# Consecutive tokens in a group of 128, v in four loads, and the gate's loads on ScalarE's queue

## The chip, the cores and the metric

The kernel runs on one core of a Trainium2 chip. The time is device microseconds of one execution, the median of several runs. A profile comes from a further, profiled execution, which has its own time. Engines are called as in the profile: PE (TensorE; PEld its weight loads), DVE (VectorE), ACT (ScalarE), POOL (GpSimd), SP (SyncE). A "q" behind an engine's name (SPq, ACTq) means the queue in which that engine issues DMAs.

## The reference

Linear attention over 8 batches, 8 heads, 576 tokens and 64 columns a head, followed by a mixture of experts over the 4608 tokens of 512 columns. Cut to what matters:

```python
def phi(x):                                    # q, k: (8, 8, 576, 64); w_phi: (64, 128)
    proj = np.einsum('bhsd,df->bhsf', x, w_phi)
    proj = proj - np.max(np.abs(proj), axis=-1, keepdims=True)
    return np.concatenate([np.exp(proj), np.exp(-proj)], axis=-1)
kv  = np.einsum('bhsf,bhsd->bhfd', phi(k), v)
z   = np.sum(phi(k), axis=2)
num = np.einsum('bhsf,bhfd->bhsd', phi(q), kv)
den = np.einsum('bhsf,bhf->bhs', phi(q), z)[..., None] + 1e-06
x   = (num / den).transpose(0, 2, 1, 3).reshape(4608, 512)

do_compute = x @ w_skip > 0                    # the other tokens are copied to the output
logits = x[do_compute] @ w_gate                # 8 experts, the best one is taken
e, g   = argmax(logits), softmax(logits)[argmax(logits)]
out[do_compute] = x + g * (relu(x @ w1[e]) @ w2[e])      # w1: (8, 512, 1024), w2: (8, 1024, 512)
```

All of it is in fp32; the expert products are made of a high and a low part of each operand.

## The kernel before

The attention part comes first, up to about 385 us of the profiled execution, and the expert part after it.

**Units and steps.** A unit is four heads of one batch, of k or of q: 16 units of k and 16 of q. A unit has five items: item 0 is the tail (64 tokens a head, 512 to 575), items 1 to 4 cover the 512 others, 1 and 2 for one half of the heads, 3 and 4 for the other. The main loop walks over steps; at each step the stages of several items run, some steps apart: load, transposing (`st_t`), projection with w_phi on PE (`st_proj`, L318), subtraction of the largest value on VectorE (L325, L328), the exponentials on ScalarE (L343, L344 for k; L370, L371 for q), products (L386 and L393 for k with v, L484 for q), and the division (`norm`, L435 to L448). The stream of q runs six steps behind that of k.

**Loads of q and k.** `st_load` (L265) issues four DMAs of 144 KB for a unit, all on SyncE's queue, in pieces of 32 columns (128 bytes) a token, so that 32 tokens lie on 32 partitions. There are four buffers for these tiles ("raw"); a load waits until the buffer's former unit has been transposed.

**Transposes.** VectorE transposes blocks of 32x32. Item 0 is one operation of 128x128 (L293); items 1 and 3 are one operation of 128x512 each (L295), which serve two items. 512 tokens are cut into four groups of 128. In the kernel before, group g holds the tokens 4p + g, p from 0 to 127. Therefore the 32 tokens of a block go to four groups, eight to each: neighbouring tokens are written 128 elements (512 bytes) apart. PE reads a group as 64 + 64 consecutive columns (L320).

**Where the group's order is seen elsewhere.** v must have the same tokens on the same partitions: `st_loadv` (L272) loads the four heads of a unit in one DMA, 256 consecutive elements (four tokens) for each partition and head; two buffers. The attention's result `xm` has token 4p + g in [p, g]; it is stored to the scratch rows (`rowm`, L502, L563) and, as the output of tokens that no expert computes, to the output (`rest`, L634). The table `kt_i` (L154 to L161) says which scratch row (first half) and which output row (second half) each [p, group] is.

**The gate.** `wgs` holds w_gate and w_skip in the layout of the products; GpSimd copies it into `aug` (L138), which is first used at step 10 (`st_aug`, L417). Its eight loads (L130, L131; 4.0 and 0.5 KB) are issued on SyncE's queue by `setup_aug` at step 6.

**Order.** The instructions of an engine run in the order of its queue. For the attention part, a planner of the language orders each engine's queue by times that it works out itself from the kernel; only PE's order is written out by hand from step 8 to 79 (CFG "man"). Changing instructions can thus reorder others. The expert part's order is written out by hand.

**The expert part.** Rows are gathered from the scratch rows by GpSimd (L214), multiplied with the weights of their expert (L887 to L919), and scattered to the output (L847). Which rows stand together in a slot follows from their rank within an expert, counted group by group and, in a group, partition by partition.

Of the kernel before, what the change touches and what calls it, by code (L numbers as in the profile page):

```python
# [18 lines left out]
P = 128  # L19
# [5 lines left out]
def kernel(  # L25
# [12 lines left out]
    nc = tc.nc  # L38
    B, H, S, D = q.shape
    NF = w_phi.shape[1]  # L40
    E = w_gate.shape[1]
    DM = H * D
    SQ = S
# [54 lines left out]
    wgs = ac.tile([P, NP2, E + 1], F32, name="wgs")  # L98
# [22 lines left out]

    ft = const.tile([P, NSL, 4], I32, name="ft")

    def setup_aug():
        for hd in range(2):
            r = slice(hd * 64, hd * 64 + 64)
            for hq in range(NQ):
                w = slice((hq * 4 + 2 * hd) * D, (hq * 4 + 2 * hd + 2) * D)
                g2 = slice(2 * hq, 2 * hq + 2)
                nc.sync.dma_start(out=wgs[r, g2, 0:E], in_=w_gate[w].rearrange("(g p) e -> p g e", p=D))  # L130
                nc.sync.dma_start(out=wgs[r, g2, E:E + 1], in_=w_skip[w].rearrange("(g p o) -> p g o", p=D, o=1))  # L131
        nc.gpsimd.memset(aug, 0.0)
        for hd in range(2):
            r = slice(hd * D, (hd + 1) * D)
            c = hd * NA1
            for g in range(NP2):
                nc.gpsimd.tensor_copy(out=aug[r, g, c:c + D], in_=ident[r, hd * D:(hd + 1) * D])
            nc.gpsimd.tensor_copy(out=aug[r, :, c + D:c + NA1], in_=wgs[r])  # L138

    def setup():  # L140
        nc.gpsimd.memset(ones_b, 1.0)
        nc.gpsimd.memset(ones_f, 1.0)
        nc.gpsimd.memset(Stot, 0.0)
        nc.gpsimd.affine_select(
            out=tri, in_=ones_b, pattern=[[1, P]], base=-1, channel_multiplier=-1,
            compare_op=ALU.is_ge, fill=0.0,
        )
        nc.gpsimd.iota(iota_p, pattern=[[1, P]], base=0, channel_multiplier=0, allow_small_or_imprecise_dtypes=True)
        nc.gpsimd.iota(desc, pattern=[[-1, E]], base=E, channel_multiplier=0, allow_small_or_imprecise_dtypes=True)
        nc.gpsimd.memset(ones_b, 1.0)  # L150
        NB2 = B // 2
        kt_i = const.tile([P, 2, NT], I32, name="kt_i")
        kv_ = kt_i.rearrange("p c (b t) -> p c b t", t=9)
        nc.gpsimd.iota(kv_[:, 0, :, 0:8], pattern=[[2 * S, NB2], [512, 2], [1, 4]], base=0, channel_multiplier=4)  # L154
        nc.gpsimd.iota(kv_[:, 0, :, 8:9], pattern=[[2 * S, NB2], [1, 1]], base=1024, channel_multiplier=1)
        nc.gpsimd.iota(
            kv_[:, 1, :, 0:8], pattern=[[2 * S, NB2], [S, 2], [1, 4]], base=0, channel_multiplier=4)
        for par in range(2):
            r = slice(par * 64, par * 64 + 64)
            nc.gpsimd.iota(  # L160
                kv_[r, 1, :, 8:9], pattern=[[2 * S, NB2], [1, 1]], base=par * S + 512, channel_multiplier=1)  # L161
        h_i = const.tile([P, 2, NT], I32, name="h_i")
        nc.vector.tensor_scalar(out=h_i[:, 1], in0=kt_i[:, 0], scalar1=127, scalar2=None, op0=ALU.bitwise_and)
        nc.vector.tensor_tensor(out=h_i[:, 0], in0=kt_i[:, 0], in1=h_i[:, 1], op=ALU.subtract)
        nc.vector.tensor_scalar(out=h_i[:, 1], in0=h_i[:, 1], scalar1=1.0, scalar2=None, op0=ALU.add)
        nc.vector.tensor_copy(out=sid, in_=kt_i[:, 1])
        nc.gpsimd.memset(ft[:, NS2:NSL, 1:2], 0)
        nc.gpsimd.memset(ft[:, NS2:NSL, 3:4], int(BIG))
        nc.vector.tensor_copy(out=ids.rearrange("p t c -> p c t"), in_=h_i)
# [58 lines left out]
    with actx:  # L228
# [7 lines left out]
        vu = v.rearrange("b h s d -> (b h) s d").rearrange("(u h) s d -> u s h d", h=4)  # L236
# [9 lines left out]
        for b in range(B):  # L246
            for kind in ("k", "q"):
                for hq in range(NQ):
                    u = Unit()
# [9 lines left out]
        def st_load(u):  # L259
            src = kv_in[u.kind]  # L260
            u.raw = ld.tile([P, 2, 18, 32], F32, tag="raw", name="raw", bufs=4)
            for hd in range(2):
                for dh in range(2):
                    r = hd * 64 + dh * 32
                    nc.sync.dma_start(  # L265
                        out=u.raw[r:r + 32].rearrange("p r t c -> p (r t) c"),
                        in_=src[u.g, hd][:, :, dh * 32:dh * 32 + 32])

        def st_loadv(u):
            u.v = ld.tile([P, 4, 4 * D], F32, tag="v", name="v")  # L270
            u.vt = vts[u.g % 2]
            nc.sync.dma_start(  # L272
                out=u.v.rearrange("p h (g c) -> p h g c", c=D).rearrange("p h g c -> p h (g c)"),
                in_=vu[u.g, 0:4 * P].rearrange("(p g) h c -> p h g c", g=4).rearrange("p h g c -> p h (g c)"))

        def st_loadvt(u):
            for pr in range(2):
# [4 lines left out]
        def st_t(u, i):  # L282
            if i == 0:
                n, sfx = P, "t"
                src = u.raw[:, :, 16:18, :].rearrange("p r t c -> p r (t c)")
            elif i in (1, 3):
                n, sfx = 4 * P, ""
                src = u.raw[:, i // 2, 0:16, :].rearrange("p t (q g) -> p t q g", g=4)
            else:
                return  # L290
            xT = hl.tile([P, n], F32, tag="xT" + sfx, name="xT" + sfx)
            if i == 0:
                nc.vector.transpose(out=xT.rearrange("p (r c) -> p r c", r=2), in_=src)  # L293
            else:
                nc.vector.transpose(out=xT.rearrange("p (g t q) -> p t q g", g=4, q=8), in_=src)  # L295
            u.hlp[(i + 1) // 2] = xT

        def st_proj():
# [213 lines left out]
        def post(b):  # L512
            last = b == B - 1
            xm, lgm = xm_of[b]
# [21 lines left out]
            for xx, lg, o, n in reversed(parts):  # L536
                nc.vector.tensor_reduce(
                    out=L[:, o:o + n, :], in_=lg.rearrange("p t h e -> p t e h"), axis=AX.X, op=ALU.add,
# [5 lines left out]
                out=key[:, 0:nt], in0=d[:, 0:nt], scalar=0.0,  # L544
# [6 lines left out]
                out=OH[:, T, :], in0=L[:, 0:nt, E:E + 1].broadcast_to([P, nt, E]), scalar=0.0, in1=oh[:, 0:nt],  # L551
# [5 lines left out]
            for xx, lg, o, n in parts:  # L557
                nc.scalar.activation(
                    out=xx[:, :, DM + 1:XW], in_=sid[:, t0 + o:t0 + o + n].rearrange("p (t o) -> p t o", o=1), func=AF.Copy)
# [11 lines left out]
            S = 4  # L571
# [60 lines left out]

            def rest():
                nc.sync.dma_start(  # L634
                    out=out[b * SQ:b * SQ + 4 * P].rearrange("(p g) m -> p g m", g=4), in_=xm[:, :, 0:DM])
                if b % 2 == 1:
                    for par in range(2):
                        o = (b - 1 + par) * SQ + 4 * P
                        nc.sync.dma_start(out=out[o:o + 64], in_=xt[par * 64:par * 64 + 64, 0, 0:DM])

            if last:
                rests.extend((rank, rest))
            else:
                for d, f in zip(CFG["post"], (rank, index, rest)):
                    later.append((now[0] + d, f))
                if b == EB:
                    for j in range(2):
                        later.append((now[0] + CFG["post"][2] + 1 + 2 * j, lambda j=j: pick(j)))
# [49 lines left out]
        for dh in range(2):  # L698
            nc.scalar.dma_start(
                out=wsrc[dh * 64:dh * 64 + 64],  # L700
                in_=w_phi)
        st_load(streams[0][1][0])

        def run_stage(lag, f):
            for items, us, off in streams:
                s = now[0] - off - lag
                if 0 <= s < n:
                    f(*items[s])
# [7 lines left out]
        def f_t():  # L716
            for items, us, off in streams:
                s = now[0] - off
                if s == CFG["ql"]:
                    st_load(us[0])  # L720
                if 0 <= s < n:
                    u, i = items[s]
                    st_t(u, i)
                    if i == 0 and s // 5 + 1 < len(us):
                        st_load(us[s // 5 + 1])
# [360 lines left out]
    def weight_regs(e):  # L1086
        r = nc.sync.value_load(e, min_val=0, max_val=E - 1)
        return bass.ds(r, 1)
# [5 lines left out]
    for grp in CFG["seq"]:  # L1094
# [7 lines left out]
        for which, w, n in how:  # L1102
            for _ in range(n):
                x = slots[which]
                c = done.get((x, w), 0)
# [42 lines left out]
    def step_at(t):  # L1148
        return sum(1 for v in T if v < t)
# [29 lines left out]
    for xs_, back in ((two, 2), (one, 1)):  # L1179
        for n, x in enumerate(xs_):  # L1180
            if x not in order[0:2]:
                free = end[xs_[n - back]] + LATE + 1 if n >= back else 0
                g = free if x[0] == "E" else max(free, made)
                at(g, lambda x=x: gather(x))
                r = max(step_at(T[g] + 8.0), step_at(T[begin[x]] - CFG["rows"]), one_done[order[order.index(x) - 2]] + 1)
                at(min(r, begin[x] - 1), lambda x=x: rows(x))
    loose[0] = True
    with tc.manual_schedule():
# [4 lines left out]
        for k, (w, x, c) in enumerate(steps):  # L1193
            kind, i = x
# [53 lines left out]
    with tc.For_i(0, nx, 1) as it:  # L1248
# [3 lines left out]
        e = weight_regs(eid[0:1, bass.ds(sl, 1)])  # L1252
# [37 lines left out]
```

## Time and profile before

| | |
|---|---|
| time, median of 3 runs | 678.85 us (678.34 to 679.5) |
| the profiled execution's own time | 674.92 us |
| its span, first to last instruction | 672.9 us |
| PE busy | 580.7 us (86%) |
| PEld busy | 474.0 us (70%) |
| DVE busy | 531.7 us (79%) |
| ACT busy | 330.7 us (49%) |
| POOL busy | 361.7 us (54%) |
| mean granted clock of PE | 0.961 |
| DMA | 108.32 MB in 220025 packets |

In the profile's rows of groups stand the line, the engine, the operation, out<-in, the sizes and the count; then the busy time in us and the mean length of one in ns; then the idle time of the engine just before them, and what ended it. In rows of the timeline stand the start and the length in us, the instruction, and in brackets the idle time of its engine before it and what ended that. An instruction of a busy engine can start shortly before the one ahead of it ends. In rows of waits of SP stand what waited, for what, and the total in us, the number of times, and the longest. In rows of windows the engines' busy times have the number of instructions in brackets.

### The profile page before, as it was taken

What the parts mean: (1) busy time and instruction counts of PE and PEld (TensorE: products, weight loads), DVE (VectorE), ACT (ScalarE), POOL (GpSimd) and SP (SyncE); (2) the same over time, 40 slices, a digit from 0 to 9 for tenths busy, and PEclk for the clock granted to TensorE, in tenths of its full rate; (3) what the DMA queues carried; (4) which work ended last, traced back from release to release, by engine and by line L of the source; (5) the groups of instructions that cost most, each with busy time, mean ns of one, the idle gap of its engine ahead of it and who ended that gap; (6) DMA issues with size and microseconds to landing.
All of it is one profiled execution on the core that took longest, in us unless ns stands there. A gap on an engine that the chain in (4) does not pass through costs nothing. (4 is left out here: it accounts for less than half of the span.)

```text
span 672.9 us, 18699 instructions
## 1 busy us (share of the span) xinstructions
PE 580.7 (86%) x7486; PEld 474.0 (70%) x7486; DVE 531.7 (79%) x1084; ACT 330.7 (49%) x649; POOL 361.7 (54%) x389
## 2 busy tenths in 40 slices
PE   3559889879889979889898989869999979999994
PEld 2347667657667766667676778859888868898893
DVE  5379879798987998898999678995777987866860
ACT  2246545445534645555455455432465745765640
POOL 3535355346545463555556365696555967168321
PEclk9959998899999999999999989998999989999997
DMA  9763575375476546754404539957658668777300
GB/s 162 132 118 69 125 175 110 80 163 129 83 183 122 138 114 130 176 121 92 152 33 139 187 108 301 336 197 256 202 190 266 223 204 283 263 229 274 129 17 28
DMA packets 220025, 108.32 MB, mean 161 GB/s; under 512 B 158625, under 2 KB 200737, under 8 KB 219936
## 3 DMA queue, kind: packets, MB, share of 16 engines
q1 hardware_dynamic: 216576, 97.59, 54.4%
q0 software_dynamic: 3200, 9.45, 4.0%
q8 instruction: 60, 0.98, 0.6%
q14 instruction: 29, 0.24, 0.1%
q10 hardware_dynamic: 160, 0.07, 0.0%
HBM read 83.86 MB, written 24.02 MB: 160 GB/s over the span
## 5 line engine op out<-in xcount | busy, mean ns | idle before, releaser
L351 POOL TENSOR_TENSOR z<-ek 128x512 f32<-128x512 f32 x64 | 81.5, 1273 | 139.4 <-ACT ek L344 104.6
L201 POOL TENSOR_TENSOR w<-wraw_c,w 128x256 fp32r<-128x256 f32 x124 | 113.5, 950 | 54.4 <-ACT w L196 54.4
L201 DVE TENSOR_TENSOR w<-wraw_c,w 128x1024 fp32r<-128x1024 f32 x65 | 95.6, 1480 | 14.5 <-ACT w L196 13.2
L196 ACT ACTIVATE w<-wraw_c 128x1024 fp32r<-128x1024 f32 x96 | 97.5, 1051 | 4.2 <-DMA wraw_c<-in_moe_w_dram 3.0
L318 PE MATMUL ps_P<-wsrc,xT 64*64 64x128 f32 x2048 | 81.8, 292 | 13.9 <-DVE xT L295 7.2
L328 DVE TENSOR_TENSOR u<-ps_P,m 128x1024 f32<-128x1024 f32 (+2 forms) x86 | 89.7, 1043 | 4.6 <-DVE m L325 0.5
L325 DVE TENSOR_REDUCE m<-ps_P 128x8 f32<-128x1024 f32 (+2 forms) x86 | 87.4, 1017 | 4.2 <-PE ps_P L318 3.9
L484 PEld LDWEIGHTS ps_O<-kva,eq 128*64 128x64 f32 x2048 | 74.7, 136 | 16.8 <-issue 6.0
L484 PE MATMUL ps_O<-kva,eq 128*64 128x74 f32 x2048 | 77.6, 228 | 4.2 <-DVE lgm L447 4.1
L318 PEld LDWEIGHTS ps_P<-wsrc,xT 64*64 64x64 f32 x2048 | 60.2, 141 | 29.7 <-issue 20.6
L386 PE MATMUL ps_K<-ek,v 128*64 128x256 f32 x512 | 72.3, 405 | 0.0
L295 DVE STREAM_TRANSPOSE xT<-raw 128x512 f32<-128x512 f32 x64 | 68.8, 1079 | 4.2 <-PE ps_P L318 2.4
L343 ACT ACTIVATE ek<-u 128x512 f32<-128x512 f32 x64 | 40.4, 631 | 59.8 <-DVE u L328 54.6
L364 PE MATMUL ps_U<-ident,u 128*128 128x128 f32 x288 | 50.6, 294 | 21.7 <-DVE u L328 11.3
L914 PE MATMUL ps_O<-w,hh 128*128 128x512 f32 x160 | 64.5, 403 | 0.0
L847 POOL DMA_INDIRECT out_dram<-o,si x22 | 30.7, 1396 | 61.4 <-DVE si L846 52.6
L370 ACT ACTIVATE eq<-ps_U 128x512 f32<-128x512 f32 x64 | 37.8, 591 | 51.9 <-PE ps_U L364 50.1
L364 PEld LDWEIGHTS ps_U<-ident,u 128*128 128x128 f32 x288 | 31.1, 144 | 32.1 <-issue 12.3
L918 PE MATMUL ps_O<-w,hh 128*128 128x512 f32 x120 | 47.8, 398 | 2.3 <-POOL w L201 2.3
L386 PEld LDWEIGHTS ps_K<-ek,v 128*64 128x64 f32 x512 | 32.0, 140 | 22.2 <-issue 12.7
L919 PE MATMUL ps_O<-w,hlo 128*128 128x512 f32 x120 | 47.3, 394 | 0.0
L293 DVE STREAM_TRANSPOSE xTt<-raw 128x128 f32<-128x128 f32 x32 | 9.8, 307 | 40.9 <-DMA raw<-in_q_dram 24.1
(259 smaller groups left out, 1235.9 us busy)
## 6 DMA issues: line engine op xcount, KB each, us to landing
wraw_c<-in_moe_w_dram SPq DMA_DIRECT2D x96, 512.0 KB, 4.8
raw<-in_k_dram SPq DMA_DIRECT2D x64, 144.0 KB, 3.1
raw<-in_q_dram SPq DMA_DIRECT2D x64, 144.0 KB, 4.0
v<-in_v_dram SPq DMA_DIRECT2D x16, 512.0 KB, 4.0
out_dram<-xm SPq DMA_DIRECT2D x8, 1024.0 KB, 5.5
xrows<-xm SPq DMA_DIRECT2D x8, 516.0 KB, 4.5
xrows<-xm SPq DMA_DIRECT2D x8, 512.0 KB, 4.8
vt<-in_v_dram SPq DMA_DIRECT2D x32, 32.0 KB, 3.5
```

What stands on the lines that cost most here:

```text
L196: nc.scalar.activation(out=hi, in_=raw, func=AF.Copy)
L201: eng.tensor_tensor(out=lo[:, r], in0=raw[:, r], in1=hi[:, r].bitcast(F32), op=ALU.subtract)
L295: nc.vector.transpose(out=xT.rearrange("p (g t q) -> p t q g", g=4, q=8), in_=src)
L318: nc.tensor.matmul(p[s * 64:s * 64 + 64, hd, (nj + j) * NF:(nj + j + 1) * NF], xT[r, g * P + s * 64:g * P + s * 64 + 64], wsrc[r], start=T ...
L325: nc.vector.tensor_reduce(out=m.rearrange("p (j h) -> p j h", h=2), in_=pv, axis=AX.X, op=ALU.max, apply_absolute_value=True)
L328: nc.vector.tensor_tensor(out=uu[:, 0:2 * nj, :].rearrange("p (j h) f -> p j h f", h=2), in0=pv, in1=m.rearrange("p (j h o) -> p j h o", h ...
L351: zeng.tensor_tensor(out=z, in0=e[:, 0:2, :], in1=e[:, 2:4, :], op=ALU.add)
L364: nc.tensor.transpose(t[:, tt * P:(tt + 1) * P], uu[:, tt, :], ident)
L386: nc.tensor.matmul(o[hd * 64:hd * 64 + 64, :], u.v[:, 2 * hd + pr, g * D:(g + 1) * D], u.e[i][:, 2 * j + hd, :], start=(g == 0), stop=False,)
L484: nc.tensor.matmul(ov[s * 64:s * 64 + 64, 2 * j + hd, :], e[:, half, j, hd, s * 64:s * 64 + 64], kva[:, half, 2 * pr + hd, :], start=(half ...
L914: nc.tensor.matmul(y[sub], hh[:, t], wh[:, fi, :], start=first, stop=False)
L918: nc.tensor.matmul(y[sub], hh[:, t], wl[:, fi, :], start=False, stop=False)
```

## The change

A group becomes 128 consecutive tokens: group g holds the tokens 128g + p. The large transpose then writes the elements in the order in which it makes them, and its input and output are viewed without the regrouping. v's load follows with one DMA a head, in pieces of one token (64 elements, 256 bytes): four DMAs of 128 KB a unit instead of one of 512 KB. The second half of `kt_i` and the store to the output follow as well; the scratch rows keep their places. The gate's eight loads are taken out of `setup_aug` into a function of their own, issued on ScalarE's queue before the main loop, behind the two loads of w_phi.

```diff
-    def setup_aug():
+    def load_gate():
         for hd in range(2):
             r = slice(hd * 64, hd * 64 + 64)
             for hq in range(NQ):
...
-                nc.sync.dma_start(out=wgs[r, g2, 0:E], in_=w_gate[w].rearrange("(g p) e -> p g e", p=D))
-                nc.sync.dma_start(out=wgs[r, g2, E:E + 1], in_=w_skip[w].rearrange("(g p o) -> p g o", p=D, o=1))
+                nc.scalar.dma_start(out=wgs[r, g2, 0:E], in_=w_gate[w].rearrange("(g p) e -> p g e", p=D))
+                nc.scalar.dma_start(out=wgs[r, g2, E:E + 1], in_=w_skip[w].rearrange("(g p o) -> p g o", p=D, o=1))
+
+    def setup_aug():
         nc.gpsimd.memset(aug, 0.0)
...
         nc.gpsimd.iota(
-            kv_[:, 1, :, 0:8], pattern=[[2 * S, NB2], [S, 2], [1, 4]], base=0, channel_multiplier=4)
+            kv_[:, 1, :, 0:8], pattern=[[2 * S, NB2], [S, 2], [P, 4]], base=0, channel_multiplier=1)
...
             u.vt = vts[u.g % 2]
-            nc.sync.dma_start(
-                out=u.v.rearrange("p h (g c) -> p h g c", c=D).rearrange("p h g c -> p h (g c)"),
-                in_=vu[u.g, 0:4 * P].rearrange("(p g) h c -> p h g c", g=4).rearrange("p h g c -> p h (g c)"))
+            for h in range(4):
+                nc.sync.dma_start(
+                    out=u.v[:, h, :].rearrange("p (g c) -> p g c", c=D),
+                    in_=vu[u.g, 0:4 * P, h, :].rearrange("(g p) c -> p g c", p=P))
...
-                src = u.raw[:, i // 2, 0:16, :].rearrange("p t (q g) -> p t q g", g=4)
+                src = u.raw[:, i // 2, 0:16, :]
...
-                nc.vector.transpose(out=xT.rearrange("p (g t q) -> p t q g", g=4, q=8), in_=src)
+                nc.vector.transpose(out=xT.rearrange("p (t c) -> p t c", c=32), in_=src)
...
                 nc.sync.dma_start(
-                    out=out[b * SQ:b * SQ + 4 * P].rearrange("(p g) m -> p g m", g=4), in_=xm[:, :, 0:DM])
+                    out=out[b * SQ:b * SQ + 4 * P].rearrange("(g p) m -> p g m", p=P), in_=xm[:, :, 0:DM])
...
         st_load(streams[0][1][0])
+        load_gate()
```

## The prediction

> **What bounds the kernel now.** First the busy time of the engines over two stretches: the steady attention part and the second half of the start.
>
> ```profile
> 40.00:360.00 320.00, 282.25 (x5183) 215.85 (x5181) 280.61 (x625) 166.44 (x388) 167.03 (x150) 0.97 0.53 120
> 20.00:40.00 20.00, 8.70 (x112) 5.14 (x112) 6.78 (x12) 3.90 (x8) 8.87 (x10) 0.76 0.72 136
> ```
>
> The columns are PE, PEld, DVE, ACT and POOL busy, granted clock, DMA share, GB/s. From 40 to 360 us VectorE (DVE) is busy 280.61 of 320 us and PE 282.25: both at 88%, and neither has much room. So the next view is the VectorE groups of that stretch with what ended their idle time (first two rows), followed by the groups of the whole run in which one operation stands at several sizes.
>
> ```profile
> L295 DVE STREAM_TRANSPOSE xT<-raw 128x512 f32<-128x512 f32 x56 | 60.8, 1086 | 2.4 <-PE ps_P L318 2.4
> L293 DVE STREAM_TRANSPOSE xTt<-raw 128x128 f32<-128x128 f32 x25 | 7.7, 308 | 25.8 <-DMA raw<-in_q_dram 18.6 <-DMA raw<-in_k_dram 5.9 <-issue 1.2
> ...
> L295 DVE STREAM_TRANSPOSE xT<-raw 128x512 f32<-128x512 f32 x64 | 68.8, 1079 | 4.2 <-PE ps_P L318 2.4 <-DMA raw<-in_k_dram 1.8
> L293 DVE STREAM_TRANSPOSE xTt<-raw 128x128 f32<-128x128 f32 x32 | 9.8, 307 | 40.9 <-DMA raw<-in_q_dram 24.1 <-DMA raw<-in_k_dram 15.5 <-issue 1.2
> L328 DVE TENSOR_TENSOR u<-ps_P,m 128x1024 f32<-128x1024 f32 x45 | 54.7, 1217 | 2.6 <-DVE m L325 0.5
> L328 DVE TENSOR_TENSOR u<-ps_P,m 128x512 f32<-128x512 f32 x9 | 6.1, 680 | 0.3
> ```
>
> VectorE's idle time is not spread evenly: 25.8 us of it stands in front of the small tail transpose L293, which waits for a load of q (18.6) or k (5.9) and, VectorE running in order, holds up everything behind it. Between those waits VectorE runs back to back, as one unit of the timeline shows (SyncE's loads of the same stretch after it).
>
> ```profile
> 203.97 1.09 DVE L295 STREAM_TRANSPOSE xT<-raw 128x512 f32<-128x512 f32 x1
> 204.91 1.21 DVE L328 TENSOR_TENSOR u<-ps_P,m 128x1024 f32<-128x1024 f32 x1
> ...
> 216.43 0.31 DVE L293 STREAM_TRANSPOSE xTt<-raw 128x128 f32<-128x128 f32 x1 [3.03 <-DMA raw<-in_q_dram]
> 216.66 0.92 DVE L328 TENSOR_TENSOR u<-ps_P,m 128x768 f32<-128x768 f32 x1
> ...
> 226.43 1.08 DVE L295 STREAM_TRANSPOSE xT<-raw 128x512 f32<-128x512 f32 x1
> ...
> 205.09 2.61 SPq L265 DMA_DIRECT2D raw<-in_k_dram  x4
> 208.71 5.31 SPq L265 DMA_DIRECT2D raw<-in_q_dram  x4
> 222.17 0.39 SPq L272 DMA_DIRECT2D v<-in_v_dram  x1
> 222.65 0.66 SPq L279 DMA_DIRECT2D vt<-in_v_dram  x1
> 227.54 2.52 SPq L265 DMA_DIRECT2D raw<-in_k_dram  x4
> ...
> SPq L265 <- DVE xT L295: 67.7, 14, 7.1
> ```
>
> This is the loop that sets the pace. The transpose of 203.97 ends at 205.06, and k's load is issued at 205.09: SyncE was waiting for its buffer (67.7 us in 14 such waits, last row). Then come k's four loads, a store and q's four loads, and the tail transpose sits until 216.43 for q. From there VectorE works without a gap to the next such transpose at 226.43. A unit is 22.46 us: 12.46 paced by loads, 9.97 by VectorE.
>
> **The transposes (the main term).** The 64 large ones take the same elements and put neighbours next to each other instead of 512 bytes apart. The nearest row with neighbouring writes is L293: 307 ns for 128 columns. L328 gives the price of one more column: (1217 - 680)/512 = 1.05 ns, and 680 - 512 x 1.05 = 142 ns fixed. L293 fits that: 142 + 128 x 1.05 = 276, and 31 ns of its own. A large one at that rate would take 307 + 384 x 1.05 = 710 ns against 1079: 0.37 us less to its end. What the next instruction sees is less: at 203.97 it starts after 0.94 us, 0.15 before the end; at 216.43 after 0.23, 0.08 before the end. So 0.94 becomes 0.71 - 0.08 = 0.63, and a large transpose saves VectorE **0.31 us**. Bounds: 0.37 above; below, nothing, if a transposed column costs 2.1 ns wherever it goes (then 128 columns are 269 ns, leaving 38 ns fixed against L328's 142, which is why I take the other end).
>
> Where this lies on the path: in a unit whose tail transpose waits for q, the loads' half starts when the last k transpose ends, 0.37 earlier; the two other large transposes in that half only lengthen the wait. The second half holds one large transpose: 0.31. Together 0.68 of a possible 1.24. Between 40 and 360 us nine units wait so, 18.6 us in all; these are the longest and the shortest wait, and two of the units without one:
>
> ```profile
> 123.25 0.31 DVE L293 STREAM_TRANSPOSE xTt<-raw 128x128 f32<-128x128 f32 x1 [3.14 <-DMA raw<-in_q_dram]
> 171.32 0.31 DVE L293 STREAM_TRANSPOSE xTt<-raw 128x128 f32<-128x128 f32 x1 [0.91 <-DMA raw<-in_q_dram]
> ...
> 149.63 0.30 DVE L293 STREAM_TRANSPOSE xTt<-raw 128x128 f32<-128x128 f32 x1
> 239.63 0.31 DVE L293 STREAM_TRANSPOSE xTt<-raw 128x128 f32<-128x128 f32 x1
> ```
>
> 9 x 0.68 = 6.1 us. Those units hold 36 of the 56 large transposes; the other 20 save 0.31 each, 6.2, less 0.6 in each of two units that wait for k instead: 5.0. PE then has its 282.25 us in 309 instead of 320. VectorE already waits 4.8 us for PE in front of L295 and L325 (2.4 each; the second from the row below), so I put half of that again on it: 2.4 lost.
>
> ```profile
> L325 DVE TENSOR_REDUCE m<-ps_P 128x8 f32<-128x1024 f32 x43 | 50.9, 1184 | 2.5 <-PE ps_P L318 2.4
> ```
>
> Steady part: 6.1 + 5.0 - 2.4 = **8.7 us**, between 0 and 60 x 0.31 = 18.6.
>
> **The gate's loads leave SyncE, v's grow there (the start).** SyncE issues nearly without a pause from 6.99 on:
>
> ```profile
> 6.99 0.70 SPq L272 DMA_DIRECT2D v<-in_v_dram  x1
> ...
> 16.82 3.38 SPq L265 DMA_DIRECT2D raw<-in_q_dram  x4
> 20.24 0.78 SPq L272 DMA_DIRECT2D v<-in_v_dram  x1
> 21.07 0.61 SPq L130 DMA_DIRECT2D wgs<-in_moe_w_gate_dram  x1
> ...
> 26.99 1.24 SPq L279 DMA_DIRECT2D vt<-in_v_dram  x2
> 28.34 2.93 SPq L265 DMA_DIRECT2D raw<-in_k_dram  x4
> 33.93 0.31 DVE L293 STREAM_TRANSPOSE xTt<-raw 128x128 f32<-128x128 f32 x1 [9.55 <-DMA raw<-in_k_dram]
> ```
>
> From 24.3 to 33.9 VectorE waits for the fourth k load, issued at 28.34. The eight gate loads in front of it fill 21.07 to 26.99: 5.92 us, which go. Two loads of v ahead of it become eight: 3 x 0.70 + 3 x 0.78 = 4.4 more. Net 1.5 us earlier. The first two q loads, between the two v loads, come 2.1 later, but the wait at 33.93 swallows that. Bounds: v's parts at 0.39 (the row of 222.17) add 2.3 and leave 3.6; at the 0.85 of one of q's four (16.82) they add 5.3 and leave 0.6. I take **1.5 us**, since queue and backlog are those of the two rows.
>
> **Edits that I cost at nothing.** On ScalarE's queue the eight gate loads follow w_phi's:
>
> ```profile
> 1.44 0.55 ACTq L699 DMA_DIRECT2D wsrc<-in_w_phi_dram  x1
> 10.93 0.63 ACT L343 ACTIVATE ek<-u 128x512 f32<-128x512 f32 x1 [7.27 <-DVE u L328]
> ```
>
> 8 x 0.6 = 4.8 us from 2.0 end at 6.8; ScalarE idles until 10.93. Without that cover they would cost 4.8. In the steady part v's three further issues take SyncE 3 x 0.48 (222.17 to 222.65) = 1.4 us more; from the end of vt at 223.31 to the k load at 227.54 SyncE waits 4.2 us anyway. Uncovered they would cost 16 x 1.4 = 22. v then lands near 227.6 instead of 226.2 (4.0 us after its issue, fifth row), and the first product with a new v stands at 230.32:
>
> ```profile
> 230.32 1.08 PE L386 MATMUL ps_K<-ek,v 128*64 128x256 f32 x8
> 221.00:225.00 4.00, 4.00 (x87) 3.11 (x86) 3.83 (x8) 2.32 (x5) 1.28 (x1) 1.00 0.30 92
> 225.00:229.00 4.00, 4.00 (x81) 3.10 (x81) 3.93 (x8) 3.03 (x8) 3.04 (x3) 1.00 0.28 71
> q1 hardware_dynamic: 2070, 0.26, 65.6%
> v<-in_v_dram SPq DMA_DIRECT2D x16, 512.0 KB, 4.0
> DMA packets 220025, 108.32 MB, mean 161 GB/s; under 512 B 158625, under 2 KB 200737, under 8 KB 219936
> ```
>
> For the transfers, v's 512 pieces of 1 KB become 2048 of 256 bytes. Of k's 128-byte pieces alone (fourth row, 227.5 to 230 us) one takes 0.656 x 2.5 x 16 / 2070 = 12.7 ns of an engine; a piece of 256 bytes lies between that and four times it, 51 ns, so a v takes 1.6 to 6.5 us on 16 engines. I take the lower third, some 2.5 us: the engines are busy 0.30 and 0.28 in the stretch where v moves, so this fits before k at 227.54. The Trainium skill, "DMA: Bandwidth & Descriptors", section Specifications, says that pieces under 512 bytes lose line rate, because they are read, modified and written; it gives no price, and by it the sum would lie towards the last rival but one. The output store is the same for the engines: it already went in pieces under 8 KB (219936 of 220025, last row), 2 KB a token. Token order inside an expert changes, the counts do not, so the expert part keeps its work.
>
> **Sum.** 8.7 + 1.5 = 10.2 us. The profiled execution took 674.92 (span 672.9 and 2.0 around it), so 664.7; the median of the runs, 678.85, stands 3.9 above it, so **668.7 us**.
>
> **Rivals.** (a) The waits do not grow, because the order of VectorE's queue, which a planner makes anew, puts the tail transpose later: all 18.6 us count and 3.6 at the start: 656.7. For it: the units of 149.63 and 239.63 show no wait for q. Against: nine do. (b) A transposed column costs 2.1 ns anyhow: only the start is left, 677.3. Against: the 38 ns. (c) The four loads of v reach into k's: at 51 ns a piece v runs from 222.17 to 228.7, past 227.54, so k, q and the tail transpose come 1.2 us later in each of 13 units, 15.6 lost against 10.2 won: 684.2. It decides from 5.4 us for a v on. Against: the 0.30 share and the 12.7 ns. This is how the rule of the Trainium skill named above would show here. (d) The planner, counting a load as earlier than it lands, puts the tail transpose one pair of L325 and L328 further forward (1.18 + 1.22 = 2.4 us): in 13 units 31 lost, less the 18.6 and 1.5: 689.8. For it: VectorE waits at L293 in most units, so the planner is already too hopeful. Against: nothing in the change makes loads look earlier than now, save the gate's absence at the start.
>
> **How the numbers follow.** Forecast 0.60 (between 662 and 675), (a) 0.15, (b) 0.07, (c) 0.08, (d) 0.10. Telling apart 0.2%, 1.4 us, is about what a measurement of this kernel can do. Faster: forecast, (a) and half of (b), 0.78; within: the other half of (b) and a corner of the forecast, 0.06; slower: (c) and part of (d), 0.16. The range takes in half of (a), (b) and the near side of (c): 657.5 to 682.
>
> **What would show it.** L295 near 710 ns with start-to-start 0.63; if still 1079, (b). The waits before L293 for q above 18.6 us although the units are shorter; if below 10, (a). The k load after the first gap issued near 26.8 instead of 28.34. v's last landing before k's issue; if k's loads land later than 3.1 us, (c). The forecast is wrong if L295 drops and the attention part, up to the last L318 at 382.5, ends less than 6 us earlier.
>
> ```profile
> L318 PE MATMUL ps_P<-wsrc,xT x2048: 268/269/473, 7.2 to 382.5; 64*64 64x128 f32 x187
> ```

## The result, and the profile after

The median went from 678.6 us (675.47 to 679.5) to **660.61 us** (655.62 to 666.6): a ratio of 0.9718, with a 95% interval of 0.9647 to 0.979. The profiled execution took 655.62 us against 674.92, 19.3 less, where the prediction had 10.2. The time lies in the range, but below the 662 to 675 to which the forecast's 0.60 was given, and nearer to rival (a) than to the forecast. The run of 666.6 us, and the profiled execution of one later kernel (the kernel before with late tails), fell in a slower state: the ratios leave such runs out, and of that profile only the attention part, at clock 1.00, is read.

To see where it went, the attention part is cut at the ninth and at the last of the 64 large transposes, which do the same work in both kernels. Timeline of the kernel before (start, length):

```profile
42.93 1.06 DVE L295 STREAM_TRANSPOSE xT<-raw 128x512 f32<-128x512 f32 x1
...
353.50 1.11 DVE L295 STREAM_TRANSPOSE xT<-raw 128x512 f32<-128x512 f32 x1
```

The view of one line of the kernel after (ns min/median/max, first and last start):

```profile
L298 DVE STREAM_TRANSPOSE xT<-raw x64: 668/701/712, 6.2 to 335.7; 128x512 f32<-128x512 f32 x64
```

The ninth stands at 32.29 after (in the timeline below). So the start ends 10.6 us earlier; the stretch from there to the last large transpose takes 303.4 us instead of 310.6, 7.2 less; and the remaining 1.3 of the span's 19.1 (672.9 to 653.8) come after it.

**The steady stretch.** Windows from the ninth to the last large transpose, first of the kernel before, then of the kernel after (PE, PEld, DVE, ACT, POOL busy, clock, DMA share, GB/s):

```profile
42.93:353.50 310.57, 274.93 (x5046) 211.13 (x5048) 271.56 (x605) 161.88 (x379) 161.60 (x145) 0.98 0.54 122
```

```profile
32.29:335.70 303.41, 270.67 (x5005) 208.41 (x5005) 257.17 (x606) 157.88 (x372) 159.99 (x144) 0.98 0.59 128
```

VectorE's groups in the same stretch of the kernel after (columns as before):

```profile
L328 DVE TENSOR_REDUCE m<-ps_P 128x8 f32<-128x1024 f32 x41 | 49.2, 1201 | 4.9 <-PE ps_P L321 4.9
L298 DVE STREAM_TRANSPOSE xT<-raw 128x512 f32<-128x512 f32 x55 | 38.5, 700 | 0.3 <-PE ps_P L321 0.3
...
L296 DVE STREAM_TRANSPOSE xTt<-raw 128x128 f32<-128x128 f32 x26 | 8.1, 310 | 32.2 <-DMA raw<-in_q_dram 23.2 <-DMA raw<-in_k_dram 8.9
```

VectorE has 14.4 us less to do (271.56 to 257.17), and half of that became idle time: 39.0 us of idle before (310.57 - 271.56) and 46.2 after. The granted clock is 0.98 in both, so it isn't what makes the difference. The place of the idle time is the one foreseen. In front of the tail transpose the waits for q and k were 18.6 + 5.9 = 24.5 us and are 23.2 + 8.9 = 32.1.

**The start.** VectorE's timeline of the kernel before, behind the tail transpose of 33.93, and then that of the kernel after:

```profile
34.17 0.92 DVE L325 TENSOR_REDUCE m<-ps_P 128x6 f32<-128x768 f32 x1
37.40 0.31 DVE L293 STREAM_TRANSPOSE xTt<-raw 128x128 f32<-128x128 f32 x1 [2.32 <-DMA raw<-in_q_dram]
```

```profile
24.34 0.31 DVE L296 STREAM_TRANSPOSE xTt<-raw 128x128 f32<-128x128 f32 x1 [1.94 <-DMA raw<-in_q_dram]
24.57 0.92 DVE L328 TENSOR_REDUCE m<-ps_P 128x6 f32<-128x768 f32 x1
25.60 0.96 DVE L331 TENSOR_TENSOR u<-ps_P,m 128x768 f32<-128x768 f32 x1
26.47 0.70 DVE L298 STREAM_TRANSPOSE xT<-raw 128x512 f32<-128x512 f32 x1
27.10 1.18 DVE L328 TENSOR_REDUCE m<-ps_P 128x8 f32<-128x1024 f32 x1
...
30.94 0.31 DVE L296 STREAM_TRANSPOSE xTt<-raw 128x128 f32<-128x128 f32 x1 [1.33 <-DMA raw<-in_k_dram]
...
32.29 0.69 DVE L298 STREAM_TRANSPOSE xT<-raw 128x512 f32<-128x512 f32 x1
```

SyncE's queue in the timeline of the kernel after, at the start and in one unit of the steady stretch:

```profile
7.17 2.58 SPq L275 DMA_DIRECT2D v<-in_v_dram  x4
...
21.69 2.38 SPq L275 DMA_DIRECT2D v<-in_v_dram  x4
...
25.52 3.05 SPq L267 DMA_DIRECT2D raw<-in_k_dram  x4
...
204.34 2.04 SPq L275 DMA_DIRECT2D v<-in_v_dram  x4
...
209.09 2.67 SPq L267 DMA_DIRECT2D raw<-in_k_dram  x4
```

The fourth k load is issued at 25.52 instead of 28.34: 2.8 us earlier, within the bounds of 0.6 to 3.6. But the ninth large transpose comes 10.6 earlier, and the timeline shows why. Before, the tail transpose that waits for this load (9.55 us, at 33.93) stood in VectorE's queue ahead of the search for the largest value over 768 columns (L325 at 34.17). After, that operation (now L328, at 24.57), the subtraction behind it, a large transpose and the first two operations of 1024 columns stand ahead of the tail transpose, and run while the load is under way; the tail then waits 1.33 us. The tail itself comes 3.0 us earlier (30.94 instead of 33.93), with the load; the other 7.7 lie between it and the ninth large transpose, 1.35 us after and 9.0 before, because work that stood behind it is now done ahead of it, and the next tail transpose, of q, no longer stands there with its wait of 2.32. VectorE's order has changed, though no line of the change speaks of it.

### The profile page after: what moved, and what is told of

It reads as the page before. It is cut to its first block, busy times and chain, and to the rows that moved or that the text cites. A ratio compares the mean times of both kernels' runs of the same rounds, so it can differ in the third digit from the quotient of the medians.

```text
span 653.8 us, 18749 instructions
## 1 busy us (share of the span) xinstructions
PE 578.6 (88%) x7486; PEld 473.8 (72%) x7486; DVE 515.1 (79%) x1084; ACT 329.4 (50%) x649; POOL 360.3 (55%) x389
## 5 line engine op out<-in xcount | busy, mean ns | idle before, releaser
L203 DVE TENSOR_TENSOR w<-wraw_c,w 128x1024 fp32r<-128x1024 f32 x65 | 86.6, 1342 | 13.1 <-ACT w L198 12.1
L328 DVE TENSOR_REDUCE m<-ps_P 128x8 f32<-128x1024 f32 (+2 forms) x86 | 88.4, 1028 | 6.0 <-PE ps_P L321 5.8
L389 PE MATMUL ps_K<-ek,v 128*64 128x256 f32 x512 | 73.9, 408 | 0.0
L367 PE MATMUL ps_U<-ident,u 128*128 128x128 f32 x288 | 49.4, 289 | 13.3 <-ACT eq L374 11.0
L367 PEld LDWEIGHTS ps_U<-ident,u 128*128 128x128 f32 x288 | 30.3, 141 | 23.5 <-ACT eq L374 12.1
L298 DVE STREAM_TRANSPOSE xT<-raw 128x512 f32<-128x512 f32 x64 | 44.5, 697 | 2.2 <-DMA raw<-in_k_dram 1.9
L905 PE MATMUL ps_P<-x,w 128*128 128x256 f32 x144 | 38.8, 299 | 4.7 <-DVE x L782 4.7
```

Of the source, the lines that this page charges most:

```text
L203: eng.tensor_tensor(out=lo[:, r], in0=raw[:, r], in1=hi[:, r].bitcast(F32), op=ALU.subtract)
L328: nc.vector.tensor_reduce(out=m.rearrange("p (j h) -> p j h", h=2), in_=pv, axis=AX.X, op=ALU.max, apply_absolute_value=True)
L367: nc.tensor.transpose(t[:, tt * P:(tt + 1) * P], uu[:, tt, :], ident)
L389: nc.tensor.matmul(o[hd * 64:hd * 64 + 64, :], u.v[:, 2 * hd + pr, g * D:(g + 1) * D], u.e[i][:, 2 * j + hd, :], start=(g == 0), stop=False,)
```

## The experiments

Ratios are times over the kernel before, run on the same chip, with 95% intervals.

**The gate's loads alone.** The kernel before, with `load_gate` as in the change and nothing else of it.

> The kernel before with one part of the change: the gate's eight loads on ScalarE's queue ahead of the loop. Tokens are grouped as before, v is one load. Theory A (the start's gain of some 10 us comes from SyncE's queue, freed of 5.92 us): the fourth k load is issued near 22.4 instead of 28.34, the ninth large transpose starts near 32 to 34 instead of 42.9, the span is 660 to 664, and a large transpose stays at 1079 ns. Theory B (the cheaper transposes bring the start's gain too, the gate only the net of 1.5 us that was forecast): span 669 to 673, ninth large transpose at 40 or later.

Measured 666.56 us, 0.9857 [0.9804, 0.991]. Its timeline, SyncE's load and then VectorE:

```profile
24.65 3.55 SPq L267 DMA_DIRECT2D raw<-in_k_dram  x4
...
25.54 0.95 DVE L327 TENSOR_REDUCE m<-ps_P 128x6 f32<-128x768 f32 x1
...
30.82 0.31 DVE L295 STREAM_TRANSPOSE xTt<-raw 128x128 f32<-128x128 f32 x1 [4.33 <-DMA raw<-in_k_dram]
```

The span, 662.8 us, is what theory A said, but not the way there. The load comes 3.7 us earlier, less than the 5.92 of the loads removed, and the ninth large transpose stands at 36.6 instead of 42.93, 6.4 earlier. Of these, 3.1 come with the load (the tail at 30.82 instead of 33.93); 1.0 because L327 of 768 columns now stands ahead of the waiting tail; and 2.3 because the next tail transpose, of q, which waited 2.32 us at 37.40 before, finds its data there at 35.23. By 0.9857 the gate's loads are worth 9.7 us of 678.6 (6.1 to 13.3), where by the prediction's reckoning they were 5.92 of the net 1.5, with 4.4 lost to v. Not all of the 9.7 is the start's: in this profile the steady stretch is 4.0 us shorter as well (306.6), though its transposes are the old ones, and why is open.

**All but the gate.** The whole change, with the gate's loads left where they were on SyncE's queue.

> The changed kernel with the gate's loads put back on SyncE's queue at step 6: consecutive tokens and v in four loads alone. Theory A: a large transpose near 697 ns, 8 us gained after the ninth large transpose, but the start gains nothing or loses up to 4.4 us (six more loads of v ahead of the fourth k load), so a span of 664 to 669. Theory B: span 655 to 658, ninth large transpose near 33.

Measured 669.51 us, 0.9875 [0.9821, 0.9929]: 8.5 us (4.8 to 12.1). By the prediction's terms this part was 8.7 for the transposes less 4.4 for v's loads at the start, 4.3. The views of the transposes' line, of SyncE's timeline and of VectorE's:

```profile
L296 DVE STREAM_TRANSPOSE xT<-raw x64: 668/702/715, 6.1 to 350.2; 128x512 f32<-128x512 f32 x64
...
30.01 2.82 SPq L265 DMA_DIRECT2D raw<-in_k_dram  x4
...
24.56 0.95 DVE L326 TENSOR_REDUCE m<-ps_P 128x6 f32<-128x768 f32 x1
...
35.37 0.31 DVE L294 STREAM_TRANSPOSE xTt<-raw 128x128 f32<-128x128 f32 x1 [9.86 <-DMA raw<-in_k_dram]
```

The start gains next to nothing here: the k load is 1.7 us later than before (30.01 to 28.34), and the ninth large transpose stands at 42.4. Yet the operation of 768 columns (L326) stands ahead of the waiting tail here too, with the gate's loads where they were; it runs at 24.56, so its data can be there long before 34.17. From the tail to the ninth large transpose it is 7.0 us instead of 9.0, but the tail itself comes 1.4 later. One operation moved is thus worth little; in the kernel after five have moved. Neither part alone gives that order, and at the start their gains (6.4 and 0.5) don't add up to 10.6. In the timed runs the two parts (0.9857 x 0.9875 = 0.9734) agree with the whole (0.9718) within the intervals. One caution: in this profile the steady stretch is only 2.8 us shorter than before, at a granted clock of 0.96 instead of 0.98 and with PE busy 278.15 us in it instead of 274.93; and kernels whose transposes are unchanged differ there too, from 306.6 (the gate alone) to 313.1 us (the order at the start alone, below). A single profile gives the steady term to some 3 us.

**v in four loads alone.** The kernel before, with

```diff
-            nc.sync.dma_start(out=u.v..., in_=vu[u.g, 0:4 * P].rearrange("(p g) h c -> p h g c", g=4)...)
+            for h in range(4):
+                nc.sync.dma_start(
+                    out=u.v[:, h, :], in_=vu[u.g, 0:4 * P, h, :].rearrange("(p g) c -> p (g c)", g=4))
```

> The kernel before with v in four loads, one a head, in pieces of 1 KB; tokens grouped as before, the gate on SyncE's queue. Theory A: the fourth k load is issued 2.3 to 5.3 us later than 28.34, the start loses about that, nothing changes later since SyncE's three further loads lie in time in which it waits: span 675 to 678. Theory C (SyncE's further loads cost in every unit): 48 loads at 0.48 us, span 685 to 695.

Measured 674.23 us, 0.9972 [0.9937, 1.0006]: no loss beyond 0.4 us, and a gain only if it is small. The fourth k load goes out at 29.22, 0.9 later than before and not 2.3 to 5.3, and the ninth large transpose stands at 41.5. That the four issues cost time, at the start or later, is out. The pieces here are of 1 KB, so this run says nothing on pieces of 256 bytes.

**VectorE's order at the start alone.** The kernel before, its loads untouched; in the first 20 steps each tail transpose is queued behind the latest subtraction.

```diff
+        sub_last = [None]
-                nc.vector.transpose(out=xT.rearrange("p (r c) -> p r c", r=2), in_=src)
+                with tc.issue_after(sub_last[0].ins) if sub_last[0] is not None and now[0] < 20 else ExitStack():
+                    nc.vector.transpose(out=xT.rearrange("p (r c) -> p r c", r=2), in_=src)
-            nc.vector.tensor_tensor(
+            sub_last[0] = nc.vector.tensor_tensor(
```

> The kernel before, but in the first 20 steps a tail transpose is queued on VectorE behind the latest subtraction (L328 of the kernel before) instead of where the planner puts it; loads, tokens and the gate are as before. Theory A (the late load sets the start): the fourth k load still goes out near 28.3 and the gain is at most 3 us, span 670 to 673. Theory D (the start's gain is VectorE's order: a tail transpose that the planner queues too early blocks work that is ready): the 9.55 us in front of the tail transpose vanish, and the span is 662 to 666.

Measured 663.81 us, 0.978 [0.9712, 0.9848]. Its timeline (VectorE, with SyncE's k load among it):

```profile
27.00 2.02 DVE L327 TENSOR_REDUCE m<-ps_P 128x6 f32<-128x768 f32 x2
27.93 2.91 SPq L266 DMA_DIRECT2D raw<-in_k_dram  x4
...
33.32 1.07 DVE L297 STREAM_TRANSPOSE xT<-raw 128x512 f32<-128x512 f32 x1
```

The fourth k load is issued at 27.93, nearly as late as before (28.34), and still the ninth large transpose comes at 33.32, 9.6 us earlier than before and within about 1 us of the kernel after. The order alone is enough; an earlier load isn't needed for it.

**All tail transposes late, after and before.** The same edit without the limit of 20 steps, on the kernel after and on the kernel before. If the order at the start is worth 10 us, the waits in front of the other tails should go the same way.

> The changed kernel with every tail transpose queued on VectorE behind the latest subtraction, in all steps. Theory D (VectorE is held up by tail transposes that the planner queues a unit ahead of their use): the 38.6 us in front of the tail transposes shrink below 15, and the span goes from 653.8 to 635 to 648. Theory E (the loop over the four buffers of q and k or PE's own work paces the steady part anyway): the waits move to the large transposes or to the reductions that wait for PE, and the span stays at 650 or above.

> The kernel before with every tail transpose queued on VectorE behind the latest subtraction, in all steps. Theory D: the 39.6 us in front of the tail transposes shrink below 15, span 650 to 660, clearly under that of the run that did so in the first 20 steps alone (663.6). Theory E: as that run, 660 to 667. Against the changed kernel in the same form this shows what the consecutive tokens bring where the order of VectorE's queue is the same: by the forecast's terms 0.31 us for each of some 60 large transposes, 18.6, if VectorE is then the bound.

On the kernel after: **629.41 us** (628.48 to 631.05), 0.928 [0.9236, 0.9325], which beats both kernels. On the kernel before: 640.13 us, 0.9414 [0.9368, 0.946]. Both are better than was expected. First rows of the kernel after with late tails (two groups of the whole run, a window, the last product with `kva`), then of the kernel before with late tails (a group, the window, the product):

```profile
L298 DVE STREAM_TRANSPOSE xTt<-raw 128x128 f32<-128x128 f32 x32 | 9.6, 301 | 0.0
L300 DVE STREAM_TRANSPOSE xT<-raw 128x512 f32<-128x512 f32 x64 | 44.8, 703 | 10.0 <-DMA raw<-in_q_dram 3.7 <-PE ps_P L323 2.4 <-DMA wgs<-in_moe_w_gate_dram 2.1
...
40.00:340.00 300.00, 289.33 (x5414) 221.97 (x5411) 276.10 (x675) 169.49 (x395) 171.35 (x156) 1.00 0.63 142
...
L489 PE MATMUL ps_O<-kva,eq x2048: 224/227/279, 38.9 to 347.2; 128*64 128x74 f32 x187
```

```profile
L295 DVE STREAM_TRANSPOSE xTt<-raw 128x128 f32<-128x128 f32 x32 | 9.6, 300 | 0.0
...
40.00:340.00 300.00, 284.08 (x5292) 216.30 (x5290) 284.51 (x660) 165.51 (x386) 169.92 (x152) 1.00 0.59 136
...
L486 PE MATMUL ps_O<-kva,eq x2048: 225/227/278, 40.7 to 357.0; 128*64 128x74 f32 x187
```

The waits in front of the tail transpose are gone (0.0); part of them has moved, for those in front of the large transposes are 10.0 us where the kernel after had 2.2. For the most part they were not the price of late data but of a place in the queue: the planner puts a tail transpose about a unit ahead of its use (in the kernel before, that of 216.43 is first used by PE at 236.29), at a time when its load is still on its way, and everything behind it on VectorE waits with it. Without them the consecutive tokens bring more than in the original order, but not all: the attention part ends 9.8 us earlier after than before (357.0 to 347.2 for the last product), of 64 x 0.31 = 19.8, and the timed ratios say 9.1 (0.9414 to 0.928 of 678.6). The window points at what is next: PE is busy 289.33 of 300 us.

**Five buffers for q and k.** The kernel after with `bufs=5` for `raw` instead of 4, so that a load need not wait for the transposes of the fourth unit back.

> The changed kernel with five buffers instead of four for the loads of q and k. Theory F (the waits in front of the tail transposes come from loads that wait for a buffer): the 38.6 us shrink below 20 and the span falls to 640 to 650. Theory D: the planner, told of a load that may start sooner, queues the tail transpose sooner as well; the waits stay above 25 us and the span within 5 us of 653.8.

Measured 646.33 us, 0.9528 [0.9471, 0.9585]. Groups of this kernel, whole run:

```profile
L296 DVE STREAM_TRANSPOSE xTt<-raw 128x128 f32<-128x128 f32 x32 | 9.7, 303 | 20.3 <-DMA raw<-in_k_dram 11.3 <-DMA raw<-in_q_dram 8.2 <-DMA v<-in_v_dram 0.6
```

The span, 643.9 us, lies where theory F put it, so an earlier load shortens the waits as well; but it leaves 20.3 us of them, and the late order leaves none. With both, the next run, there is nothing to add.

> The changed kernel with every tail transpose queued behind the latest subtraction and five buffers for the loads of q and k. Theory D, in which the buffers only matter because tail transposes are queued too early: no further gain, span 625 to 630. Theory F (loads that wait for a buffer cost by themselves): span 615 to 622.

Measured 629.82 us, 0.9295 [0.9256, 0.9334], the same as with four buffers. The buffers mattered only because the tails were queued early.

**The gate's loads with the order held.** The kernel after with late tails, and the gate's loads back on SyncE's queue.

> The changed kernel with every tail transpose queued behind the latest subtraction, and the gate's loads put back on SyncE's queue at step 6. VectorE's order is nearly that of the same kernel with the gate on ScalarE's queue (span 627.6), so this shows what the queue alone is worth. Theory A (SyncE's queue sets the start): the fourth k load goes out 5 us later, the ninth large transpose starts 4 to 6 us later than 32.1, span 631 to 634. Theory D (the order is what counted; a load a few us later is still early enough): span 626 to 630, ratio to the kernel before within 0.005 of 0.928.

Measured 635.31 us, 0.9346 [0.9299, 0.9392]. SyncE's k load, a large transpose, the last product, and then a place in the expert part on VectorE, GpSimd and PE:

```profile
29.94 2.89 SPq L266 DMA_DIRECT2D raw<-in_k_dram  x4
31.07 0.70 DVE L298 STREAM_TRANSPOSE xT<-raw 128x512 f32<-128x512 f32 x1
...
L487 PE MATMUL ps_O<-kva,eq x2048: 225/227/278, 39.2 to 347.6; 128*64 128x74 f32 x187
...
394.07 0.46 DVE L1035 TENSOR_TENSOR tm<-OH,cf 128x288 f32<-128x288 bf16 x1
395.05 8.26 DVE L1035 TENSOR_TENSOR tm<-OH,cf 128x288 f32<-128x288 bf16 x1
...
394.76 8.23 POOL L201 TENSOR_TENSOR w<-wraw_c,w 128x256 fp32r<-128x256 f32 x12
...
404.45 0.79 PE L922 MATMUL ps_O<-w,hlo 128*128 128x512 f32 x1 [7.70 <-DVE hlo L796]
```

The k load is issued at 29.94, some 3.5 us later than with the gate on ScalarE's queue (26.48), and the ninth large transpose (31.07) is not later than there (31.83); the attention part ends 0.4 us later (347.6 to 347.2). So once VectorE's order is good, the gate's queue is worth nearly nothing there. The span, 636.6 against 627.6, is still 9.0 us longer, above both theories. Most of it goes with the 7.70 us that PE waits up to 404.45, in a collision of VectorE and GpSimd (below), far from the start; PE's granted clock from 400 to 410 us is then 0.52, against 0.91 in the other kernel. By the ratios the two kernels differ by 4.5 us; whether the runs without a profile had this collision is not known.

**What an element's place costs.** In the kernel after, ahead of the loop, transposes and additions of 128x512 whose results nobody uses, three of each: output in order (pflat), neighbours 512 bytes apart as in the kernel before (pfar), pairs (ppair) or fours (pquad) kept together, neighbours 32 bytes apart (pnear); an addition in order (cflat) and with neighbours 512 bytes apart (cfar).

> The changed kernel with 15 transposes of 128x512 and 6 additions of 128x512 on scratch tiles ahead of the loop, three of each kind in a row; their results are not used. Theory G (a write next to the one before is cheap, one far from it dear): written in order 700 ns; all neighbours 512 bytes apart 1080; in pairs or fours of neighbours with the groups 512 bytes apart close to 700; neighbours 32 bytes apart like 512. If distance counts and not adjacency, 32 bytes apart costs as written in order. An addition that writes 512 bytes apart shows whether this belongs to transposes alone: with Theory G it is dearer than the one in order by the same 380 ns.

VectorE's groups from 0 to 60 us:

```profile
L757 DVE STREAM_TRANSPOSE pnear<-psrc 128x512 f32<-128x512 f32 x3 | 3.1, 1035 | 0.0
L747 DVE STREAM_TRANSPOSE pfar<-psrc 128x512 f32<-128x512 f32 x3 | 3.1, 1025 | 0.0
L745 DVE STREAM_TRANSPOSE pflat<-psrc 128x512 f32<-128x512 f32 x3 | 2.0, 682 | 1.1 <-POOL psrc L734 1.1
L749 DVE STREAM_TRANSPOSE ppair<-psrc 128x512 f32<-128x512 f32 x3 | 2.0, 670 | 0.0
L761 DVE TENSOR_SCALAR cfar<-psrc 128x512 f32<-128x512 f32 x3 | 2.0, 666 | 0.0
L753 DVE STREAM_TRANSPOSE pquad<-psrc 128x512 f32<-128x512 f32 x3 | 2.0, 658 | 0.0
L759 DVE TENSOR_SCALAR cflat<-psrc 128x512 f32<-128x512 f32 x3 | 1.2, 398 | 0.0
```

Pairs are enough (670 ns), and 32 bytes apart costs as much as 512 (1035 and 1025). The addition far apart takes 666 ns against 398 in order, 268 more and not the 380 that were expected. By an estimate with the prediction's fixed 142 ns, it falls back to one element in about 1 ns, (666 - 142)/512, and the transpose to one in 1.7, (1025 - 142)/512. This kernel's total, 673.59 us, says nothing on the change: the added work made the planner set the start's order anew, with a wait of 4.74 us for k at 32.00.

## Why the prediction was right or wrong

- **Which way, and the transposes' price: right.** 697 ns instead of 1079 was forecast as 710; from one large transpose to the next instruction 0.63 us (26.47 to 27.10), as forecast. Rival (b) is out, and so is its lower bound: far writes cost, near ones don't.
- **The steady part, 8.7: right in mechanism, and in size as far as can be told.** It is 7.2 us in the profile of the kernel after, but 2.8 in that of all but the gate, and such a figure is good to some 3 us. (A slip in the working: VectorE's half of the unit shown is 226.43 - 216.43 = 10.0 us, not 9.97, and the upper bound counts 60 large transposes where the stretch has 56; nothing hangs on either.) The waits for q were to rise above 18.6 and are 23.2. The loss to PE was put too high: VectorE's waits for PE in front of L298 and L328 are 5.2 us, where they were 4.8 (L295, L325), so they grew by 0.4 and not 2.4; the waits for loads took more in its place.
- **The start, 1.5: the step that failed.** "Net 1.5 us earlier" was not far off for the load (2.8; v's parts cost 3.5 more and not 4.4: 2.58 + 2.38 against 0.70 + 0.78). The failure is that the term was reckoned from SyncE's issues alone, with VectorE's order taken as fixed. The stretch is 10.6 us shorter, of which 3.0 go with the load and 7.7 with the order. The 9.55 us in front of 33.93 were treated as a wait for data; they were a wait of ready work behind one early-queued instruction, as the order alone showed (9.6 us with the load issued at 27.93).
- **Rival (a) had the cause, in the wrong place.** "The planner makes VectorE's order anew and puts the tail transpose later" happened at the start, where the prediction gave it 3.6 us at most; in the steady part the waits it was to hold at 18.6 grew. That the time lies near its 656.7 is thus partly chance, and that it lies in the range is owed to the range, which took in half of (a): the forecast's terms alone give 668.7, 8.1 us too much.
- **Rival (c): no.** The four loads of v take 2.04 us to issue in a unit, and end at 206.38 ahead of k at 209.09. The landings in the view of DMA issues of the kernel after:

```profile
raw<-in_k_dram SPq DMA_DIRECT2D x64, 144.0 KB, 3.1
v<-in_v_dram SPq DMA_DIRECT2D x64, 128.0 KB, 2.7
```

k's loads land after 3.1 us as before, v's after 2.7, and four issues cost nothing (0.9972). So no loss from v's short pieces shows, at a DMA share of 0.59. The price of one piece was not measured: whether the lower third of the bounds was right is not known, and for their upper end, four times the 12.7 ns, the prediction has no row.
- **Rival (d): its premise was right, its conclusion wrong.** The planner is too hopeful about loads: the waits at the tail could be had back by order alone (0.9414). But nothing in the change made it more so.
- **The gate as an edit that costs nothing: right on ScalarE's queue.** Its last load is issued by 7.83, later than the 6.8 that was reckoned, and the first exponential starts at 9.60, when the subtraction before it on VectorE ends (8.88 + 0.69), instead of 10.93. Timeline of the kernel after:

```profile
7.23 0.60 ACTq L131 DMA_DIRECT2D wgs<-in_moe_w_skip_dram  x1
...
8.88 0.69 DVE L331 TENSOR_TENSOR u<-ps_P,m 128x512 f32<-128x512 f32 x1
...
9.60 0.63 ACT L346 ACTIVATE ek<-u 128x512 f32<-128x512 f32 x1 [6.71 <-DMA wgs<-in_moe_w_skip_dram]
```

The bracket names the gate's load, whose issue had ended 1.8 us before; but the exponential works on the subtraction's output, which ends 0.03 us ahead of it, much as in the kernel before (10.23 + 0.66 to 10.93). What was missed is what the change does to the planner's order.
- **The expert part unchanged: right,** 1.3 us of the 19.1.

What stays open: how the planner works out its times, and so why the whole change moves five operations ahead of the waiting tail where each of its parts moves one. That VectorE's order is worth the start's gain is shown (the order at the start alone), why the planner chose it isn't.

## What to carry to other kernels

Where a long wait for a load stands in front of an instruction, ask first whether what is queued behind it was ready: if so, the cheap remedy is the order of the queue, not an earlier load (here 0.9414 for one rule of order, against 0.9718 for the whole change). If a planner orders the queues, a change to one queue can reorder another, so compare the order of the bottleneck's instructions in both traces before any term is put down to the change itself. On VectorE, lay out an fp32 transpose so that at least two neighbouring elements are written together.

## What the hardware showed beside

- **Adjacency in pairs is all this transpose of 128x512 in fp32 needs:** 670 ns with pairs, 682 in order, 1025 to 1035 without neighbours. The Trainium skill, "SBUF — State Buffer", section "Door 1: The DMA port swizzle (why `[64,N]` ≈ `[32,N]`)", says that a 16-byte line of SBUF needs at least two accesses in a row for full bandwidth; the trace agrees for the transpose. The addition loses less when its neighbours are 512 bytes apart (666 against 398 ns); whether that is the same price or the loss of a faster rate isn't shown, since it was not run with pairs.
- **One VectorE instruction can be held through many of GpSimd's.** L1035 took 0.46 us at 394.07 and 8.26 at 395.05, beside twelve GpSimd subtractions in a row of 8.23 us together; PE then waited 7.70. The Trainium skill, same page, section "SBUF: two separate sides", says that a VectorE instruction with two inputs in SBUF and a GpSimd instruction that reads SBUF share a port pair, and that the one that starts first keeps it for its whole instruction. The trace agrees that they hold each other up, but VectorE was not let in here between one GpSimd instruction and the next. It isn't always so. In the same kernel with the gate on ScalarE's queue, VectorE's subtractions beside such a run were let in, at 1.77 us instead of 1.23, while GpSimd's eleven took 15.71 us:

```profile
395.13 1.77 DVE L203 TENSOR_TENSOR w<-wraw_c,w 128x1024 fp32r<-128x1024 f32 x1
```

What decides between the two is open.
